# One level of Strassen's method for half of the up products of a spectral MLP kernel

## The chip, the cores and the metric

The kernel runs on one core of one Trainium2 chip. TensorE (PE; its weight loads are listed as PEld) multiplies matrices into PSUM, VectorE (DVE), ScalarE (ACT) and GpSimd (POOL) work on tiles in SBUF, and SyncE (SP) issues nearly all DMAs. The metric is the time of one execution in microseconds on the device. Before the change the median of three runs is 363.61 us (363.41 to 364.26).

## What is computed

The input x has 2048 rows of 512 numbers. Each row is normalized, and the result is the sum of x, a filter in the frequency domain and a two-layer network:

```
xn  = (x - mean) / sqrt(var + 1e-5)
A   = irfft2(rfft2(xn) * (w_r + 1j * w_i))          # over rows and columns
h   = xn @ w1 + b1                                  # w1: 512 x 1792
act = h * tanh(softplus(h))                         # Mish
out = x + A + act @ w2                              # w2: 1792 x 512
```

Inputs and outputs are float32. Every product of matrices is done with float16 pairs: a number is split in a high and a low half, and three matmuls (high x high, high x low, low x high) are added up in PSUM.

## The kernel before

The 2048 rows are four groups g of 512. F = 1792 is 14 blocks f of 128 (NFC). For each pair (g, f), numbered n = 14 g + f, there are four steps. up(n) (line 711) forms 128 x 512 values of h, transposed, in one PSUM bank: four blocks of the inner dimension times three passes, twelve matmuls of 512 columns (L727), with w1t as weights and the transposed rows xnT[g] as moving operand. mish(n) takes the bank on ScalarE (L738) into a tile hb, a_hi(n) writes the high half of the activation on ScalarE (L747), a_lo(n) the low half on VectorE (L750). down(n) (line 754) adds twelve matmuls of 512 columns to the four banks of group g. When a group is done, mlp_end(g) adds its four banks to the output rows (L792). The up products have two PSUM banks (pool ps_h), the down sums four (ps_a), the filter two (ps_f).

The filter is stream A: a first transform of the rows (s1, before), then for c = 0 to 3 the units p2_unit (psP), spectrum (products dre, dim, then some twenty operations on VectorE and GpSimd per half, ending in u, L424 and L425), dp_unit (psA) and ip_pair (psT), whose results go through memory (d_t) to the inverse s1_inverse and s1_inverse_pair (psY), near the end.

The program has two parts. In opening() and middle() the order of the instructions on every engine is the order in which they are written (tc.manual_schedule()). middle() interleaves down(0) to down(19) and up(14) to up(24) with the rows of groups 1, 2 and 3: row_in (normalized rows, high half on ScalarE, low half on GpSimd, L249), r.turn (a transposing DMA into xnT, L253), r.fold (sums and differences of row pairs for the transform, L230 to L235) and row_pair (the transform). The largest filter weight is looked for by max_wm (L443). After that a planner orders the work from priorities and its own costs. Two generators run against each other: mlp_rest (line 796) gives up or down steps, and stream_a gives steps of the filter; the list HALVES says how many up or down steps follow each step of the filter. mlp_rest keeps five activations between up and down. Some first matmuls of the filter are kept in program order.

DMAs wait in one queue on SP, in order. Tiles of one tag share a ring of buffers.

Of the kernel before, what the change touches and what calls it, by code (L numbers as in the profile page):

```python
# [41 lines left out]
def spectral_mlp_kernel(ctx, tc, x, wt, w0, w1, b1, w2, cT, cIT, cM, out):  # L42
# [21 lines left out]
    d_t = dp.tile([2, 64, 2, 32, 256], F16, tag="d_t", name="d_t")  # L64

# [46 lines left out]
    def turned(t, a):  # L112
        v = t.rearrange("p (b a e) -> p a b e", b=2, a=2)[:, a]
        return v[:, :, ::-1] if a else v

    def s1_mm_pair(k, eo, ps):
        psr = [t.rearrange("p (b a e) -> p a b e", b=2, a=2) for t in ps]
        for a in range(2):
# [3 lines left out]
                lambda r, c, h: turned(eo[c][:, h, :], a),  # L122
# [20 lines left out]

    class Rows:

        def __init__(self, g, x4):
# [5 lines left out]
            self.xT = xnT[g] = cp.tile([P, 2, 4, 512], F16, tag=f"xnT{g}", name=f"xnT_{g}")  # L152
            self.xh, self.xs, self.eo = {}, {}, {}
# [73 lines left out]
        def fold(self, j, engines):  # L227
# [4 lines left out]
            eo = self.eo[j] = [qp.tile([P, 2, D], F16, tag="q1", name=f"eo{q}_{self.g}_{j}") for q in range(2)]  # L232
            for q, v in ((0, t), (1, b)):
                nc.scalar.copy(eo[q][:, 0, :], v)
                engines[2 + q].tensor_sub(eo[q][:, 1, :], v, eo[q][:, 0, :])  # L235

        def full(self, s):
# [8 lines left out]
            )  # L246

# [16 lines left out]

    def pow2_of(name, am, n=1, out_tag=None):

        cl = sp.tile([P, n], F32, tag=f"cl{n}", name=f"cl_{name}", bufs=2)
        nc.vector.tensor_scalar(cl, am, 2.0**-60, None, op0=ALU.max)
        p2 = cp.tile([P, n], F32, tag=f"p2_{name}", name=f"p2_{name}")
        nc.vector.tensor_single_scalar(p2.bitcast(I32), cl.bitcast(I32), 0x7F800000, op=ALU.bitwise_and)  # L270
        return p2

    def scalars(name, src, factor, recip=False):
        o = cp.tile([P, 1], F32, tag=f"sc_{name}", name=f"sc_{name}")
        if recip:
            nc.vector.reciprocal(o, src)
            src = o
        nc.vector.tensor_scalar(o, src, factor, None, op0=ALU.mult)
        return o
# [67 lines left out]
    def w1_hi(k, a=0, b=2):  # L347
# [3 lines left out]
        )  # L351

# [81 lines left out]
    def load_w0():  # L434
        wmt[8] = sp.tile([P, 4, 2, 64], F32, tag="w0t", name="w0t")
# [4 lines left out]
    def max_wm(c):  # L440
        if c == 0:
            sc["mxw"] = sp.tile([P, 9], F32, tag="mxw", name="mxw")
        nc.vector.tensor_reduce(  # L443
            sc["mxw"][:, c : c + 1],
            wmt[c] if c == 8 else wmt.pop(c),
            axis=AX.XYZ if c == 8 else AX.X,
            op=ALU.max,
            apply_absolute_value=True,
        )
# [1083 lines left out]
```

## Time and profile before

| | |
|---|---|
| median of the runs | 363.61 us |
| span of the profiled execution, first to last instruction | 361.6 us |
| PE busy | 353.9 us (98%) |
| DVE busy | 278.5 us (77%) |
| ACT busy | 187.7 us (52%) |
| POOL busy | 47.8 us (13%) |
| bytes moved by DMA | 54.98 MB |

The page of the profile gives the profiled execution's time as its span; the runs are timed around the whole execution, so what lies before the first and after the last instruction is in them and not in the span. A row of a group reads: line, engine, operation, tiles written <- read, shapes, how often; then busy time and the mean of one in ns; then the engine's idle time ahead of these and what ended it. Rows by time give the start, the duration and the instruction. Rows by stretch give, for each engine, the busy time and the number of instructions in that stretch, then the granted clock, the DMA share and GB/s. A matmul's duration includes its way through the array; matmuls in a row start closer together than they last.

### The profile page before, as it was taken

To read this page: it belongs to the slowest core of one execution; us is meant where nothing else is said; L and a number is where in the kernel's file an instruction comes from. 1 tells how busy PE (TensorE), PEld (TensorE's weight loads), DVE (VectorE), ACT (ScalarE), POOL (GpSimd) and SP (SyncE) were. 2 spreads that over 40 slices of the span, in tenths; PEclk is the share of its full clock that TensorE was granted. 3 is DMA by queue.
4 is the path that set the end of the run, shared out by engine and by line. 5 is a ranking of instruction groups with operands and counts; after the bars stand their busy time and mean duration, and the time that the engine had idled before them with its cause. 6 is when DMAs were issued, how large, how long until landed. Compare 5 with 4: busy or idle time off the path is not lost.

```text
span 361.6 us, 6167 instructions
## 1 busy us (share of the span) xinstructions
PE 353.9 (98%) x2283; PEld 174.0 (48%) x2283; DVE 278.5 (77%) x543; ACT 187.7 (52%) x288; POOL 47.8 (13%) x49
## 2 busy tenths in 40 slices
PE   7999999999999999999999999999999999999994
PEld 2544444444444444545554445544554445444453
DVE  4898998886598776399998955996498933349995
ACT  5989974564654751525454365355443554445511
POOL 0020002303304500033030301130032000000000
PEclk9999999999999999999999999999999999999999
DMA  8945753699796657443611327218831524686566
GB/s 269 319 145 181 190 126 89 125 220 255 119 309 127 143 169 178 172 111 88 227 31 51 97 57 233 61 52 215 228 96 41 130 58 111 124 248 219 118 153 197
DMA packets 60702, 54.98 MB, mean 152 GB/s; under 512 B 16720, under 2 KB 49776, under 8 KB 60544
## 3 DMA queue, kind: packets, MB, share of 16 engines
q1 hardware_dynamic: 60192, 54.06, 56.6%
q10 hardware_dynamic: 480, 0.52, 0.5%
q8 instruction: 18, 0.29, 0.3%
q14 instruction: 12, 0.10, 0.1%
HBM read 34.61 MB, written 12.58 MB: 131 GB/s over the span
## 4 chain that ended last, share of the span: by engine, by line
PE 90%; DVE 6%; ACT 1%; DMA 1%; issue 0%; DVEq 0%
PE ph L727 39%; PE pa L68 13%; PE pa L71 12%; PE pa L72 12%; PE psT L672 2%; PE psS L108 1%; PE psY L108 1%; DMA x<-in_x_dram 1%; PE psA L68 1%; PE psA L71 1%; PE psA L72 1%; PE psP L516 1%; PE psP L526 1%; DVE u L425 1%; PE psP L519 1%; DVE xh L188 1%
## 5 line engine op out<-in xcount | busy, mean ns | idle before, releaser
L727 PE MATMUL ph<-xnT,w1t 128*128 128x512 f16 x672 | 153.4, 379 | 0.0
L727 PEld LDWEIGHTS <-w1t 128*128 128x128 f16 x672 | 64.6, 98 | 77.7 <-issue 2.7
L738 ACT ACTIVATE hb<-ph,b1t,fp_exp 128x512 f32<-128x512 f32 x56 | 43.2, 771 | 58.3 <-PE ph L727 58.2
L68 PE MATMUL pa<-w2t,a 128*128 128x512 f16 x181 | 68.7, 380 | 0.0
L71 PE MATMUL pa<-w2t,a 128*128 128x512 f16 x181 | 68.6, 379 | 0.0
L72 PE MATMUL pa<-w2t,a 128*128 128x512 f16 x181 | 68.6, 379 | 0.0
L750 DVE SCALAR_TENSOR_TENSOR a<-hb,ip_a,a 128x512 f16<-128x512 f32 x46 | 34.4, 749 | 34.4 <-ACT a L747 34.2
L747 ACT ACTIVATE a<-hb,ip_a 128x512 f16<-128x512 f32 x46 | 33.1, 720 | 2.3 <-DVE ip_a L288 1.2
L72 PEld LDWEIGHTS <-a 128*128 128x128 f16 x190 | 18.6, 98 | 21.0
L68 PEld LDWEIGHTS <-a 128*128 128x128 f16 x190 | 18.6, 98 | 20.8 <-issue 2.0
L71 PEld LDWEIGHTS <-a 128*128 128x128 f16 x190 | 18.6, 98 | 18.6
L249 POOL TENSOR_TENSOR xh<-xs,xh 128x512 f16<-128x512 f32 x12 | 15.4, 1292 | 56.7 <-ACT xh L223 23.4
L424 ACT ACTIVATE u<-w,sc_u 128x512 f16<-128x512 f32 x16 | 10.8, 713 | 22.1 <-DVE w L625 10.2
L531 DVE SCALAR_TENSOR_TENSOR z<-psP,z 128x512 f16<-128x512 f32 x16 | 10.8, 688 | 9.6 <-ACT z L530 9.6
L223 ACT ACTIVATE xh<-x,nb,rs 128x512 f16<-128x512 f32 x12 | 9.6, 806 | 13.1 <-DVE nb L217 11.7
L695 DVE SCALAR_TENSOR_TENSOR tt<-psT,tt 128x512 f16<-128x512 f32 x16 | 10.4, 683 | 7.3 <-ACT tt L694 7.3
L600 POOL TENSOR_TENSOR w<-X,wE 128x512 f32<-128x512 f32 x4 | 5.1, 1274 | 69.6 <-DVE X L593 69.6
L694 ACT ACTIVATE tt<-psT 128x512 f16<-128x512 f32 x16 | 8.8, 589 | 10.7 <-PE psT L672 8.8
L649 ACT ACTIVATE at<-psA 128x512 f16<-128x512 f32 x16 | 9.2, 589 | 9.4 <-PE psA L72 7.0
L156 DVE BATCH_NORM_STATS2 st<-x 128x6 f32<-128x512 f32 x16 | 10.3, 679 | 4.4 <-DMA x<-in_x_dram 4.4
L425 DVE SCALAR_TENSOR_TENSOR u<-w,sc_u,u 128x512 f16<-128x512 f32 x16 | 11.4, 747 | 2.4 <-ACT u L424 2.2
L530 ACT ACTIVATE z<-psP 128x512 f16<-128x512 f32 x16 | 9.4, 590 | 5.3 <-PE psP L526 5.2
(220 smaller groups left out, 576.7 us busy)
## 6 DMA issues: line engine op xcount, KB each, us to landing
d_y<-y SPq DMA_DIRECT2D x16, 256.0 KB, 4.2
wm<-in_wt_dram SPq DMA_DIRECT2D x8, 512.0 KB, 5.2
ai<-at SPq DMA_DIRECT2D x64, 64.0 KB, 2.2
d_t<-tt SPq DMA_DIRECT2D x32, 128.0 KB, 2.5
w1s<-in_w_dram SPq DMA_DIRECT2D x7, 512.0 KB, 9.0
w2s<-in_w_dram SPq DMA_DIRECT2D x7, 512.0 KB, 3.4
x<-in_x_dram SPq DMA_DIRECT2D x12, 256.0 KB, 7.4
yt<-d_y SPq DMA_DIRECT2D x6, 512.0 KB, 4.1
```

The lines of the kernel that those rows point to most:

```text
L68: first = nc.tensor.matmul(ps, stat(0), mov(0), start=start, stop=False)
L71: nc.tensor.matmul(ps, stat(0), mov(1), start=False, stop=False)
L72: nc.tensor.matmul(ps, stat(1), mov(0), start=False, stop=stop)
L249: engine.tensor_sub(self.xh[s][:, 1, :], self.xs[s], self.xh[s][:, 0, :])
L424: nc.scalar.activation(dst_h, src, AF.Copy, scale=scale)
L425: nc.vector.scalar_tensor_tensor(dst_l, src, scale, dst_h, op0=ALU.mult, op1=ALU.subtract)
L531: nc.vector.scalar_tensor_tensor(zl, psv, 2.0**-14, zh, op0=ALU.mult, op1=ALU.subtract)
L695: nc.vector.scalar_tensor_tensor(tt[:, :, 1, :], ps[r], 2.0**-12, tt[:, :, 0, :], op0=ALU.mult, op1=ALU.subtract)
L727: nc.tensor.matmul(ph[n + k], w1t[:, hw, dc, f * P : (f + 1) * P], xnT[g][:, hx, dc, :], start=(hw, hx, dc) == (0, 0, 0), stop=(hw, hx, dc ...
L738: nc.scalar.activation(hbt[n], ph.pop(n), AF.Mish, bias=b1t[:, f : f + 1], scale=s_exp[part_of(f)])
L747: nc.scalar.activation(act[n][:, 0, :], hbt[n], AF.Copy, scale=sc["a"])
L750: nc.vector.scalar_tensor_tensor(act[n][:, 1, :], hbt.pop(n), sc["a"], act[n][:, 0, :], op0=ALU.mult, op1=ALU.subtract)
```

## The change

The up products of groups 0 and 1 stay. For groups 2 and 3 (n from 28 on), one level of Strassen's method, in Winograd's form, is used: the 512 rows of a group are two halves of 256 (each half is one row of every pair), the 512 inner numbers are two halves, and the two blocks f = 2k and 2k + 1 of w1 are the other factor. Instead of eight products of 256 columns there are seven (six matmuls each: three passes times two inner blocks), on sums of row quarters (S1 to S4) and of weight quarters (T1 to T4).

unit(g, ks) does two such k at once, or one for the last, in four phases on two banks a and b. After each phase comes a down step. Banks are emptied and added on the way by ScalarE copies and VectorE sums:

```diff
+        with tc.manual_schedule(engines={PE}):
+            a, b = (ps_h.tile([P, n, 256], F32, tag="h", name=f"ph{c}_{g}_{ks[0]}") for c in "ab")
+            products(a, g, ks, "B11", "A11", True)
+            products(b, g, ks, "B21", "A12", True, True)
+        h1, h2 = (
+            mp.tile([P, n, 2, 256], F32, tag="hb", name=f"h{c}_{g}_{ks[0]}", bufs=2) for c in "12"
+        )
+        with tc.high_priority():
+            nc.scalar.copy(h1[:, :, 0, :], a)
+            nc.vector.tensor_add(h1[:, :, 0, :], h1[:, :, 0, :], b)
+        yield
+        with tc.manual_schedule(engines={PE}):
+            products(a, g, ks, "T2", "S2", False)
+            products(b, g, ks, "T1", "S1", True)
+        with tc.high_priority():
+            nc.scalar.copy(h2[:, :, 0, :], a)
+        yield
+        with tc.manual_schedule(engines={PE}):
+            products(a, g, ks, "T3", "S3", False)
+        with tc.high_priority():
+            nc.scalar.copy(h2[:, :, 1, :], a)
+            nc.vector.tensor_add(h2[:, :, 1, :], h2[:, :, 1, :], b)
+        yield
+        with tc.manual_schedule(engines={PE}):
+            products(a, g, ks, "T4", "A22", False, True)
+            products(b, g, ks, "B22", "S4", False, True)
...
+        for j in range(n):
+            mish_of(h1[:, j, 0, :], h1[:, j, 0, :], j, 0)
+        with tc.high_priority():
+            for j in range(n):
+                mish_of(h1[:, j, 1, :], a[:, j, :], j, 0)
+            nc.vector.tensor_add(h2[:, :, 0, :], h2[:, :, 0, :], b)
...
```

After the fourth phase come the Mish, a_hi and a_lo of all four blocks. mlp_rest runs the units:

```diff
+        for g in (2, 3):
+            for ks in ((0, 1), (2, 3), (4, 5), (6,)):
+                for k in ks:
+                    load_w1t(g, k)
+                last = g == 2 and ks[-1] == 6
+                for i, _ in enumerate(unit(g, ks)):
+                    if last:
+                        for name in ("A", "S", "O", "DT")[i]:
+                            load_ops(name)
+                    if len(ks) > 1:
+                        yield 1
+                        down_next()
+                    else:
+                        down_next((0, 1) if i % 2 == 0 else (2, 3))
+                    yield 1
```

The sums of the weights are made once from a second load of w1, on GpSimd, split in halves on ScalarE and VectorE, and stored in memory (d_w); each unit loads them again through a ring of three buffers:

```diff
+    def sums_w1(k, engine):
+
+        q = w1qs[k]
+        b11, b12, b21, b22 = q[:, 0:2, :P], q[:, 0:2, P:], q[:, 2:4, :P], q[:, 2:4, P:]
+        engine.tensor_sub(b11, b12, b11)
+        engine.tensor_sub(b12, b22, b12)
+        engine.tensor_sub(b22, b22, b11)
+        engine.tensor_sub(b21, b21, b22)
+
+    def store_w1t(k):
+        q = w1qs.pop(k)
+        th = cp.tile([P, 2, 4, 2 * P], F16, tag="T", name=f"wh_{k}", bufs=3)
+        split(th[:, 0], th[:, 1], q, sc["w1", w1_part(k)])
+        nc.sync.dma_start(d_w[k], th.rearrange("p h c f -> p (h c f)"))
+
+    def load_w1t(g, k):
+        wring[g, k] = cp.tile([P, 2, 4, 2 * P], F16, tag="T", name=f"wt_{g}_{k}", bufs=3)
+        nc.sync.dma_start(wring[g, k].rearrange("p h c f -> p (h c f)"), d_w[k])
```

Blocks 0 to 4 are done between the steps of middle(), 5 and 6 in stream A's first p2 units. The rows of groups 2 and 3 get their sums in middle() too, and go transposed into operands A, D, S, T, O; those of group 3 wait in memory (d_r) and are loaded, transposing, during group 2's last unit:

```diff
+        def sums(self, j):
+
+            a, b, sf = self.xs[2 * j], self.xs[2 * j + 1], self.sf
+            nc.vector.tensor_add(sf[:, 0, :], b[:, :256], b[:, 256:])
+            nc.vector.tensor_sub(sf[:, 1, :], sf[:, 0, :], a[:, :256])
+            nc.vector.tensor_sub(sf[:, 2, :], a[:, 256:], sf[:, 1, :])
+            nc.scalar.copy(self.sp[:, :, 0, :], sf)
+            nc.gpsimd.tensor_sub(self.sp[:, :, 1, :], sf, self.sp[:, :, 0, :])
```

Four of the eight maxima of the filter weights become sums of squares on ScalarE, and all are compared as squares:

```diff
-        nc.vector.tensor_reduce(
-            sc["mxw"][:, c : c + 1],
-            wmt[c] if c == 8 else wmt.pop(c),
-            axis=AX.XYZ if c == 8 else AX.X,
-            op=ALU.max,
-            apply_absolute_value=True,
-        )
+        t, m = wmt[c] if c == 8 else wmt.pop(c), sc["mxw"][:, c : c + 1]
+        if c != 8 and c % 2 == 0:
+            nc.scalar.activation(t, t, AF.Square, accum_out=m)
+            return
+        nc.vector.tensor_reduce(m, t, axis=AX.XYZ if c == 8 else AX.X, op=ALU.max, apply_absolute_value=True)
+        nc.vector.tensor_mul(m, m, m)
```

The residual rows of group 2 go to the ring "big" and are loaded when down(38) is done, the inverse's last four inputs are loaded later, and the tiles hb are two of double size instead of four. HALVES is unchanged.

More of the change, by code (lines that the diff above doesn't have):

```diff
@@ L794, in mlp_end @@
                 store_out(g, s, r)
[L796 to L810 removed]
+    STRASSEN = 2 * NFC
@@ L811, in mlp_rest, with down_next @@
+    def mlp_rest(n_up, n_down, lag):
+        def down_next(part=range(4)):
+            nonlocal n_down
+            down(n_down, part)
+            if 3 in part:
                 if n_down % NFC == NFC - 1:
@@ L1230, in row_in @@
     def row_in(r, s):
+        if r.g > 1 and s % 2:
+            r.hi_second(s)
+            r.full(s)
+            r.lo_second(s, POOL)
+            r.sums(s // 2)
+            return
         r.hi(s)
@@ L1325, in middle @@
             q.stats(s)
+        sums_w1(1, POOL)
         act_of(18)
```

296 lines of the change are left out of this document (226 added, 70 removed).

## The prediction

> **What bounds the kernel now.** I read the page's first part and its chain of waits, then the costliest groups, then the tensor engine's rows in order of time, then busy times stretch by stretch.
>
> ```profile
> span 361.6 us, 6167 instructions
> PE 353.9 (98%) x2283; PEld 174.0 (48%) x2283; DVE 278.5 (77%) x543; ACT 187.7 (52%) x288; POOL 47.8 (13%) x49
> PE 90%; DVE 6%; ACT 1%; DMA 1%; issue 0%; DVEq 0%
> ```
>
> TensorE is busy for 98% of the span and holds 90% of the chain, so a matmul that is left out is worth its place in the queue, if nothing else becomes late. The 77% of VectorE is a mean over very unequal stretches. In the next rows the columns are the stretch, its length, then PE, PEld, DVE, ACT and POOL busy.
>
> ```profile
> 82.00:140.00 58.00, 58.00 (x350) 26.69 (x349) 44.92 (x88) 29.26 (x44) 14.00 (x16) 1.00 0.77 181
> 153.70:182.40 28.70, 28.36 (x169) 14.09 (x167) 27.59 (x59) 11.36 (x20) 5.89 (x4) 1.00 0.44 134
> 182.40:211.90 29.50, 29.50 (x198) 15.26 (x195) 25.85 (x45) 14.58 (x24) 5.90 (x4) 1.00 0.28 73
> 211.90:223.30 11.40, 11.40 (x93) 6.06 (x92) 4.04 (x7) 5.24 (x10) 0.00 (x0) 1.00 0.51 134
> 223.30:251.10 27.80, 27.80 (x181) 14.14 (x179) 25.79 (x45) 13.99 (x23) 5.89 (x4) 1.00 0.38 109
> 251.10:261.60 10.50, 10.50 (x90) 5.61 (x88) 3.94 (x6) 5.07 (x9) 0.00 (x0) 1.00 0.92 239
> 261.60:288.60 27.00, 27.00 (x168) 13.22 (x166) 25.48 (x47) 12.29 (x20) 5.44 (x4) 1.00 0.38 91
> 288.60:320.30 31.70, 31.70 (x211) 15.03 (x209) 10.21 (x16) 12.85 (x20) 0.00 (x0) 1.00 0.46 107
> 323.10:357.90 34.80, 33.72 (x286) 17.78 (x284) 34.12 (x70) 13.24 (x20) 0.00 (x0) 1.00 0.66 186
> ```
>
> The first row is the hand-ordered middle. The four spectrum stages (153.7, 182.4, 223.3 and 261.6 on) leave VectorE 1.1, 3.6, 2.0 and 1.5 us idle; between them lie lighter stretches. In the last row, the inverse transforms and the ends of the sums, VectorE is free for 0.7 us in 34.8. So there are two engines near their limit, and the change relieves one and loads the other.
>
> **The TensorE saving.** The mean of 379 ns of a 512-column matmul includes its drain; what counts is the distance of starts.
>
> ```profile
> 346.01 0.38 PE L72 MATMUL pa<-w2t,a 128*128 128x512 f16 x1
> 346.23 0.27 PE L68 MATMUL psY<-yi_w,cITt 128*128 128x256 f16 x1
> ...
> 346.77 0.27 PE L72 MATMUL psY<-yi_w,cITt 128*128 128x256 f16 x1
> 346.88 0.38 PE L68 MATMUL pa<-w2t,a 128*128 128x512 f16 x1
> ```
>
> ```profile
> 159.59 2.60 PE ph L727 x12
> 175.25 1.42 DVE u L425 x2
> 176.66 0.61 DVE z L531
> ```
>
> Six 256-column matmuls take 346.88 - 346.23 = 0.65 us, 0.109 each; twelve of 512 take 2.60, 0.216 each. Half the columns cost half the time. Groups 2 and 3 have 28 blocks, 28 x 12 = 336 matmuls of 512, 336 x 0.216 = 72.6 us. They become 2 groups x 7 column pairs x 7 products x 6 = 588 matmuls of 256, 588 x 0.109 = 64.1. The saving is 8.5; with unrounded starts (0.2157 and 0.1092) 8.3, which I use. It comes at 1.18 per unit of two column pairs, nearly all of it in the third phase, which has only one product, and 0.59 in a unit of one.
>
> The other cost on this engine is 588 - 336 = 252 more weight loads.
>
> ```profile
> L727 PEld LDWEIGHTS <-w1t 128*128 128x128 f16 x672 | 64.6, 98 | 77.7 <-issue 2.7 <-ACT w1t L349 0.3
> ```
>
> ```profile
> 288.98 0.22 PE L68 MATMUL psA<-cMt,u 128*128 128x128 f16 x1
> ...
> 289.37 0.22 PE L71 MATMUL psA<-cMt,u 128*128 128x128 f16 x1
> ```
>
> psA has a fresh weight load for every 128-column matmul, and eight of them lie 289.37 - 288.98 = 0.39 us apart from first to last, 0.056 each. Loads of 98 ns are hidden even there, so I cost them at nothing under 0.109. If that cover is gone, each shows at most its 98 ns, 24.7 us in all. The Trainium skill (TensorE: Matmul & The Clock Gate, Part 3) says that a weight load overlaps running matmuls only when the row groups differ, which full-array products never do; by that rule the 24.7 us would be due. The 0.056 us spacing disagrees with it here.
>
> **What is added.** Durations come from these rows.
>
> ```profile
> L249 POOL TENSOR_TENSOR xh<-xs,xh 128x512 f16<-128x512 f32 x12 | 15.4, 1292 | 56.7 <-ACT xh L223 23.4 <-DVE xs L239 18.8 <-DMA cTt<-in_cT_dram 14.1
> L750 DVE SCALAR_TENSOR_TENSOR a<-hb,ip_a,a 128x512 f16<-128x512 f32 x46 | 34.4, 749 | 34.4 <-ACT a L747 34.2
> L888 DVE TENSOR_TENSOR m<-m,ys 128x512 f32<-128x512 f32 x12 | 7.9, 684 | 0.3 <-ACT ys L878 0.3
> L592 DVE TENSOR_TENSOR X<-dre,es 128x256 f32<-128x256 f32 x8 | 3.4, 422 | 6.7 <-ACT er L560 5.8 <-ACT es L553 0.9
> L355 DVE SCALAR_TENSOR_TENSOR w1t<-w1s,ip_w,w1t 128x1024 f16<-128x1024 f32 x7 | 9.0, 1283 | 1.0 <-ACT w1t L349 1.0
> L443 DVE TENSOR_REDUCE mxw<-wm 128x1 f32<-128x1024 f32 x8 | 9.5, 1210 | 0.0
> L601 DVE TENSOR_TENSOR w<-X,wO 128x512 f32<-128x512 f32 x4 | 5.9, 1486 | 0.0
> L603 DVE TENSOR_TENSOR w<-w,w 128x512 f32<-128x512 f32 x8 | 5.5, 684 | 0.1
> L694 ACT ACTIVATE tt<-psT 128x512 f16<-128x512 f32 x16 | 8.8, 589 | 10.7 <-PE psT L672 8.8 <-DMA ai<-at 1.9
> ```
>
> *Middle.* VectorE gets 12 row sums (0.42, 5.0), five low halves of the weight sums (1.28, 6.4), and loses four maxima to ScalarE (1.21, 4.8): +6.6 on 44.9, where 13.1 are free. GpSimd gets five blocks of four 256-wide subtractions (half of 1.29 each, 12.9) and the wide low halves of the row sums, less four shorter ones: some +18 on 14.0. L601, which runs beside a GpSimd product, takes 1.49 for work that L603 does in 0.68, so GpSimd company can double a VectorE operation with two inputs. Such operations fill about half of the 58 us (four folds of four operations at L603's 0.68, 11; the sums, 5.0; the weights' low halves, 6.4; nine a_lo, 6.7): half of the added 18 is up to 9 more. With 6.6 + 9 = 15.6 against 13.1 the middle could be 2.5 late. I take 0, since five activations lie ahead of the down products, each worth 2.60 us of TensorE's work, and keep 0 to +3. The Trainium skill (SBUF — State Buffer, Who interferes with whom) states it as a lock: a two-input VectorE instruction and a GpSimd instruction that reads block each other fully. L601 against L603 agrees; if all 18 us were met by it, an estimate, the middle would be late by 11.
>
> *Spectrum stages.* Each full unit adds three sums of 128x512 from a bank (0.68 by L888; L592 shows that reading a bank is no dearer) and three ScalarE copies (0.59, ScalarE is half idle). Its four low halves a_lo (0.75) come together after the fourth phase instead of one by one. By the places of the ups in the plan of before: stage one +2 sums, +1.28 for the low half of weight block 6, -3 a_lo = +0.4; stage two +4 sums, +2.6; stage three +2 sums, three half ones, one a_lo more, +3.3; stage four +3 sums, +2.0. TensorE's share shrinks by 1.2, 1.2, 1.8 and 1.2. VectorE then needs 28.0, 28.4, 29.1, 27.5 us where TensorE needs 27.5, 28.3, 26.0, 25.8: short by 0.5, 0.1, 3.1 and 1.7, 5.4 together. Work that isn't urgent can slip into the light stretches (7.4, 6.6 and 21.5 us idle), but the sums and the bank evictions can't. I take a third, 1.8; bounds 0 and 5.4.
>
> *Between the streams.*
>
> ```profile
> 307.82 6.85 SPq L700 DMA_DIRECT2D d_t<-tt  x8
> 316.61 1.92 SPq L857 DMA_DIRECT2D yi_z<-d_t  x4
> ```
>
> The last store of d_t is issued at 314.7 and the first reload at 316.6; the inverse begins at 320.3, right behind it. Up products lie over this transfer; the short third phase falls there, so TensorE arrives 1.2 early. I take half, 0.6; bounds 0 and 1.2.
>
> *Tail.* After 323 VectorE gets one full sum (0.68), three half ones (1.27) and, because the last full unit's four a_lo now come after its fourth phase, three more of them (2.25, at 0.67 by their spacing 2.0): 3.7 in all, with 0.7 free. What TensorE saves there (0.6) is worth nothing then. +3.0; bounds 0 and 3.7.
>
> *Transfers.*
>
> ```profile
> wE<-in_wt_dram SPq DMA_DIRECT2D x4, 512.0 KB, 5.7
> ```
>
> Fourteen 512 KB reloads of weight sums are new, some behind a ring slot that frees only after the fourth phase before; the second phase needs them 2.6 + 2.6 + 2.6 = 7.8 us later. At 5.7 they are hidden by 2.1. Each reload waits on SP's queue, with the spectrum's transfers behind it. I cost it at 0; if the cover is gone, up to 2 per unit.
>
> **Sum.** 361.6 - 7.7 (the saving ahead of the tail) + 1.8 + 0.6 + 3.0 = 359.3 us of span. The runs' median is 363.61, 2.0 above this execution's span; I leave that as it is: 361.3.
>
> **The rivals.**
>
> *All of it arrives (0.13).* The planner slips VectorE's work into its idle time in the tail too: 363.6 - 8.3 = 355.3, or 358.3 with the tail's 3.0 paid. For it: 98% PE. Against: the tail's 0.7 us.
>
> *VectorE becomes the bound (0.28).* Place: the spectrum stages and the tail; price: 5.4 + 1.2 + 3.7 and up to 3 in the middle, 10.3 to 13.3 against 7.7: 366.2 to 369. It decides slower once the waits ahead of the tail exceed 4.7. For it: the chain already runs through VectorE before 177 (the rows at 175.25 and 176.66 above). Against: the seven rows from 153.7 to 320.3 hold 43.6 us of idle VectorE against 8.3 us added.
>
> *Banks and buffers are held too long (0.13).* A unit keeps two banks and both h buffers for four phases; between third and fourth lie only a down product's 2.6 us for a 0.59 copy.
>
> ```profile
> ACT u L424 <- DVE w L625: 10.2, 2, 5.2
> ```
>
> ScalarE can stand 5.2 us behind a VectorE wait, and the copy behind it then stops TensorE for 5.2 + 0.6 - 2.6 = 3.2. Once in most stages costs about 3 us over the sum: 363.5 to 365, no change or a little slower.
>
> *The short matmuls cost more than half (0.02)*, by visible weight loads: 363.6 - 8.3 + 24.7 = 380.
>
> **How the numbers follow.** The forecast has the remaining 0.44, with 359.5 to 363 as its own range. What a measurement of this kernel tells from no change is 0.2%, 0.7 us. Faster: 0.13 and 0.41 of the forecast's, 0.02 of the banks', 0.56; same: 0.03, 0.06 of the banks', 0.04 of VectorE's, 0.13; slower: 0.24 + 0.05 + 0.02 = 0.31. The range 357.0 to 367.5 reaches to both sides.
>
> **What would show it.** Right: matmuls of 128x256 on w1 spaced 0.109 us, PE gaps gathered in the spectrum stages, DVE over 34 in the last 35 us, that stretch longer by 3. Wrong: no PE gaps at all (355), gaps right before the phases' first matmuls with ScalarE as releaser (banks), gaps before 140 (GpSimd), gaps released by weight reloads (the ring).

## The result and the profile after

The changed kernel takes 420.05 us (418.8 to 420.58) where the kernel before, beside it, takes 363.62: a ratio of 1.154, with an interval of 1.152 to 1.157. I had predicted 361.3, with a range up to 367.5. The forecast was wrong in sign, and the upper end of the range was missed by 52.6 us.

From the page of the changed kernel: the span, busy times, the slices of PE and of the granted clock (40 slices of 10.4 us, in tenths), and the chain of work that ended last.

```profile
span 417.0 us, 6930 instructions
PE 363.9 (87%) x2535; PEld 203.6 (49%) x2535; DVE 311.3 (75%) x585; ACT 216.4 (52%) x345; POOL 75.8 (18%) x81
PE   8999999999399879866699899989958989979794
PEclk9999999999979989989989999999997999999999
DVE 32%; PE 21%; DMA 14%; ACT 13%; issue 7%; POOL 7%; SPq 5%; DVEq 0%; ACTq 0%; POOLq 0%
```

TensorE, 98% busy and 90% of the chain before, is 87% busy and 21% of the chain. VectorE's share of its span even fell (77% to 75%). So no engine took TensorE's place as the bound. The chain now hops between six engines and queues. Its members wait for one another, and the holes in the PE line begin in the eleventh slice, at 104 us, inside the hand-ordered middle.

Two rows of the tensor engine in order of time, the first forward product psP and the first inverse product psY, show how late each is. Of the kernel before:

```profile
143.76 0.22 PE L68 MATMUL psP<-cMt,yt 128*128 128x128 f16 x1
...
320.29 0.85 PE L108 MATMUL psY<-yi_z,cITt 64*64 64x256 f16 x24
```

Of the changed kernel:

```profile
163.45 0.23 PE L70 MATMUL psP<-cMt,yt 128*128 128x128 f16 x1 [0.47 <-DMA yt<-d_y]
...
373.61 0.30 PE L110 MATMUL psY<-yi_z,cITt 64*64 64x256 f16 x2 [2.25 <-DMA yi_z<-d_t]
```

The middle is 19.7 us late. Between it and the inverse another 33.6 are lost: psP of the second column block begins 29.6 us late, that of the third 38.3, that of the fourth 40.3, psY 53.3. The last matmul starts at 411.55 against 356.61, 54.9 late. The largest losses thus lie in the middle, in the first two spectrum stages and just before the inverse.

The waits of the changed kernel between 95 and 165 us (waiter, what it waits for; us in total, times, longest):

```profile
POOL w1q L419 <- DMA w1q<-in_w_dram: 21.0, 4, 9.8
ACT wh L505 <- POOL w1q L422: 14.2, 4, 4.9
DVE wh L506 <- ACT wh L505: 10.4, 4, 5.8
...
PE psS L110 <- ACT eo L263: 4.6, 4, 1.8
...
PE pa L70 <- DVE m L888: 3.4, 1, 3.4
```

In the kernel before, the same view of TensorE is empty from 95 to 150 us. The first three lines are one chain: GpSimd waits for a load, ScalarE for GpSimd, VectorE for ScalarE. TensorE's 4.6 us for eo stand behind it, as the next rows show. The 3.4 us in the last line needn't come from that load: without any weight sums the same wait is 2.8 us in e1 and 3.0 in e5 below, and 0.5 in e11, which has no row sums either. The order of time of the changed kernel shows one pass of the chain (start, length, engine; in brackets the idle time before and what ended it):

```profile
94.00 1.26 SPq L157 DMA_TRANSPOSE xT<-zr  x1
...
95.31 0.58 SPq L413 DMA_DIRECT2D w1q<-in_w_dram  x1
...
99.85 0.72 POOL L419 TENSOR_TENSOR w1q<-w1q 128x256 f32<-128x256 f32 x1 [3.43 <-DMA w1q<-in_w_dram]
...
102.95 0.67 POOL L292 TENSOR_TENSOR zr<-xs,zr 128x256 f16<-128x256 f32 x1
103.02 1.15 ACT L505 ACTIVATE wh<-w1q,ip_w 128x1024 f16<-128x1024 f32 x1 [3.71 <-POOL w1q L422]
103.57 1.64 POOL L301 TENSOR_TENSOR zr<-zr 128x768 f16<-128x768 f32 x1
...
104.08 0.76 ACT L822 ACTIVATE hb<-ph,b1t,fp_exp 128x512 f32<-128x512 f32 x1
104.20 2.09 DVE L506 SCALAR_TENSOR_TENSOR wh<-w1q,ip_w,wh 128x1024 f16<-128x1024 f32 x1 [5.76 <-ACT wh L505]
...
104.89 2.75 PE L809 MATMUL ph<-xnT,w1t 128*128 128x512 f16 x12 [1.57 <-ACT hb L822]
...
108.78 0.62 ACT L263 CAST eo<-xe 128x512 f16<-128x512 f32 x1 [2.22 <-DVE xe L251]
...
109.45 0.27 PE L110 MATMUL psS<-eo,cTt 64*64 64x256 f16 x1 [1.81 <-ACT eo L263]
```

The first weight block is issued on SP only at 95.31, behind transposing loads. GpSimd stands 3.43 us for it, and the rows' low halves (L292, L301) stand behind its four subtractions. ScalarE has stood 3.71 us for GpSimd, VectorE 5.76 for ScalarE, with everything that the hand order places behind them. Behind ScalarE's wh stands the Mish at 104.08, and TensorE's up product waits 1.57 us for it; behind VectorE's wh stands xe, and TensorE's transform waits 1.81 us for eo.

### The profile page after: what moved, and what is told of

The parts are those of the page before. It is cut to its first block, busy times and chain, and to the rows that moved or that the text cites. A ratio compares the mean times of both kernels' runs of the same rounds, so it can differ in the third digit from the quotient of the medians.

```text
span 417.0 us, 6930 instructions
## 1 busy us (share of the span) xinstructions
PE 363.9 (87%) x2535; PEld 203.6 (49%) x2535; DVE 311.3 (75%) x585; ACT 216.4 (52%) x345; POOL 75.8 (18%) x81
## 4 chain that ended last, share of the span: by engine, by line
DVE 32%; PE 21%; DMA 14%; ACT 13%; issue 7%; POOL 7%; SPq 5%; DVEq 0%; ACTq 0%; POOLq 0%
DMA wt<-d_w 4%; PE pha L898 4%; PE phb L898 3%; PE pa L70 3%; PE pa L73 3%; PE pa L74 3%; DMA yi_z<-d_t 2%; ACT a L831 2%; DMA w1q<-in_w_dram 2%; DVE a L834 2%; DVE st L177 2%; DVE y L135 2%; DVE w2t L500 1%; ACT wh L505 1%; DVE wh L506 1%
## 5 line engine op out<-in xcount | busy, mean ns | idle before, releaser
L809 PE MATMUL ph<-xnT,w1t 128*128 128x512 f16 x336 | 75.7, 379 | 3.7 <-ACT hb L822 3.6
L898 PEld LDWEIGHTS <-wt 128*128 128x128 f16 x336 | 32.7, 100 | 15.3 <-DMA wt<-d_w 4.4
L961 ACT ACTIVATE h<-h,b1t,fp_exp 128x256 f32<-128x256 f32 (+1 forms) x28 | 18.7, 702 | 15.3 <-DVE h L941 11.7
L834 DVE SCALAR_TENSOR_TENSOR a<-h,ip_a,a 128x512 f16<-128x512 f32 x28 | 20.8, 767 | 7.4 <-ACT a L831 7.1
L822 ACT ACTIVATE hb<-ph,b1t,fp_exp 128x512 f32<-128x512 f32 x28 | 21.4, 765 | 4.7 <-PE ph L809 3.9
L834 DVE SCALAR_TENSOR_TENSOR a<-hb,ip_a,a 128x512 f16<-128x512 f32 x18 | 14.5, 809 | 9.3 <-ACT a L831 8.9
L505 ACT ACTIVATE u<-w,ip_u 128x512 f16<-128x512 f32 x16 | 10.7, 714 | 20.5 <-DVE w L707 9.4
L506 DVE SCALAR_TENSOR_TENSOR wh<-w1q,ip_w,wh 128x1024 f16<-128x1024 f32 x7 | 9.8, 1399 | 15.2 <-ACT wh L505 15.2
L831 ACT ACTIVATE a<-h,ip_a 128x512 f16<-128x512 f32 x28 | 19.4, 717 | 0.3
L70 PE MATMUL psA<-cMt,u 128*128 128x128 f16 x64 | 11.8, 224 | 8.5 <-DVE at L732 8.5
```

The costliest lines, as they stand in the source:

```text
L70: first = nc.tensor.matmul(ps, stat(0), mov(0), start=start, stop=False)
L505: nc.scalar.activation(dst_h, src, AF.Copy, scale=scale)
L506: nc.vector.scalar_tensor_tensor(dst_l, src, scale, dst_h, op0=ALU.mult, op1=ALU.subtract)
L809: nc.tensor.matmul(ph[n + k], w1t[:, hw, dc, f * P : (f + 1) * P], xnT[g][:, hx, dc, :], start=(hw, hx, dc) == (0, 0, 0), stop=(hw, hx, dc ...
L822: nc.scalar.activation(hbt[n], ph.pop(n), AF.Mish, bias=b1t[:, f : f + 1], scale=s_exp[part_of(f)])
L831: nc.scalar.activation(act[n][:, 0, :], hbt[n], AF.Copy, scale=sc["a"])
```

## What the idle gaps cost beside their length

The tensor engine's rows after one such gap, changed kernel:

```profile
115.08 0.59 PE L70 MATMUL pa<-w2t,a 128*128 128x512 f16 x1 [3.37 <-DVE m L888]
115.46 0.63 PE L73 MATMUL pa<-w2t,a 128*128 128x512 f16 x1
...
119.70 0.38 PE L74 MATMUL pa<-w2t,a 128*128 128x512 f16 x1
119.92 0.38 PE L809 MATMUL ph<-xnT,w1t 128*128 128x512 f16 x1
```

And the busy times around it (stretch, length, PE, PEld, DVE, ACT, POOL, then the granted clock, the DMA share and GB/s), changed kernel:

```profile
109.40:112.80 3.40, 1.31 (x24) 0.78 (x24) 3.32 (x7) 3.15 (x6) 0.00 (x0) 1.00 0.95 277
112.80:119.70 6.90, 4.62 (x12) 1.62 (x11) 6.80 (x17) 2.37 (x4) 3.23 (x4) 0.51 1.02 314
```

After 3.37 us without a matmul the starts lie 0.43 us apart instead of 0.216, until 119.70, where the 0.22 returns. The granted clock is 0.51 from 112.8 to 119.7. The Trainium skill (TensorE: Matmul & The Clock Gate, Part 1: The HAM clock gate) says that the array drops to half its clock after about one idle window of 3.4 us and needs a busy window of the same length to come back. The half clock agrees with these rows, the idle window doesn't: the clock fell at 112.8, 1.1 us into the pause, after 3.4 us in which TensorE had still been busy for 1.31. In e5, below, it fell with no long pause at all, after three holes of 0.59 to 0.75 us:

```profile
124.60:128.00 3.40, 1.45 (x12) 0.60 (x14) 3.15 (x5) 2.42 (x4) 3.40 (x5) 1.00 0.37 134
128.00:131.40 3.40, 3.40 (x25) 1.57 (x25) 3.01 (x5) 1.42 (x3) 2.17 (x6) 0.50 0.01 2
```

So short holes close together are enough. I counted every matmul of 256 or 512 columns after the start-up that is followed without a pause at 1.85 to 2.1 times the usual distance: 47 in the changed kernel and none in the kernel before. Their excess is 7.1 us. At most an eighth of the loss is thus idle time's aftermath; how much of it reaches the span isn't measured.

## The experiments

Theory Q: the loss comes from the preparation, through engines and a DMA queue that work in order. Theory V: VectorE has become the bound. Theory B, later H: TensorE waits for the up banks. Theory R: the row sums' own arithmetic is late in the middle. The expectations name the others. Most of these kernels leave a part of the computation out or put other data in its place, as the text on each says, so their times measure parts and aren't versions. Each was timed beside the kernel before (363.5 to 363.7 us in the four groups of runs). Behind the middle the planner orders each of these kernels anew, so a difference there holds its new order too.

**e1, no weight sums.** Loading, summing, splitting, storing and reloading of the weight sums are left out; the products that need them take plain blocks of w1.

```diff
 def load_w1q(k):
+    return
 def sums_w1(k, engine):
+    return
 def store_w1t(k):
+    return
...
-                w = lambda h, dc: t[:, h, c0 + dc, o : o + P]
+                w = lambda h, dc: w1t[:, h, c0 + dc, 2 * k * P + o : 2 * k * P + o + P]
```

> Leaves out the weight sums altogether: no second load of w1, no subtractions on GpSimd, no split and store, no reloads; the units read plain blocks of w1t in their place, so the result is not the reference's. TensorE's work, the row sums, the bank copies and VectorE sums of the units stay. Theory Q (queues: the middle and the first spectrum stage wait in order behind load, GpSimd, ScalarE, VectorE, store and reload of the weight sums): nearly all of the 56 us goes, 362 to 375. Theory V (VectorE is overloaded by the units' sums): only the seven low halves of 1.28 leave VectorE, 405 to 412. Theory B (banks and h buffers held by a unit): the units are the same, 410 or more outside the middle, so 395 to 405.

Measured 388.62 us, ratio 1.069 (1.066 to 1.072): 31.4 back, more than V and B allowed and 13.6 short of Q's range. The weight sums are the larger part of the loss and not nearly all of it.

**e2, sums stored but not reloaded.** Only the fourteen reloads go, and the products that need them take plain blocks of w1 as in e1:

```diff
-                for k in ks:
-                    load_w1t(g, k)
```

> Weight sums are made and stored as in the changed kernel, but never loaded again: the units read plain blocks of w1t, so the result is not the reference's. Theory Q: the preparation costs some 20 us in the middle and up to 20 in the first spectrum stage, the reloads the rest; so 395 to 408. If the reloads were the cause instead of the preparation: 370 or less. Theories V and B: 412 to 420, as before.

Measured 413.1 us, 1.136 (1.133 to 1.140). The reloads cost 420.05 - 413.1 = 7.0 us, and making and storing the sums 413.1 - 388.6 = 24.5. The time lies in the range that V and B gave, above Q's: Q had put more on the reloads. Where the 24.5 arise, psP's first rows tell: in e1 it begins at 152.37, in e2 at 163.66, so 11.3 us are lost in the middle. At the second column block it is 175.87 against 196.80, another 9.6 by the end of the first spectrum stage, in which weight blocks 5 and 6 are made.

**e3, e1 without the staging of group 3's operands**, which reads group 2's instead:

```diff
 def operand(g, name):
+    g = 2
...
-            else:
-                o, w = OPERANDS[name]
-                nc.sync.dma_start(d_r[j, :, o : o + w], src)
...
-                        for name in ("A", "S", "O", "DT")[i]:
-                            load_ops(name)
```

> As the kernel without weight sums, and besides nothing of group 3's row operands goes through memory: no stores of them in the middle, no transposing loads in group 2's last unit; group 3's units read group 2's operands, so the result is not the reference's. If the ten transposing loads of 1.2 us each on SP's queue delay the filter's weights (the GpSimd product waited 28 us for one), this is 6 to 13 us faster than without the weight sums alone; if not, within 2 us of it.

Measured 383.33 us, 1.054 (1.051 to 1.058): the staging costs 5.3, a little under the 6 that I had set as the sign of it. What it does to the queue shows in the changed kernel's DMA issues on SP:

```profile
283.13 3.74 SPq L157 DMA_TRANSPOSE xA<-d_r  x2
...
295.99 2.52 SPq L157 DMA_TRANSPOSE xD<-d_r  x2
298.61 2.52 SPq L157 DMA_TRANSPOSE xT<-d_r  x2
301.18 0.58 SPq L432 DMA_DIRECT2D wt<-d_w  x1
301.86 2.60 SPq L782 DMA_DIRECT2D d_t<-tt  x4
304.50 0.61 SPq L582 DMA_DIRECT2D wE<-in_wt_dram  x1
```

A transposing load, of 256 or 128 KB here, holds SP for 1.26 us against 0.58 for a plain load of 512 KB. Ten of them, the spectrum's stores between and one reload stand ahead of the last stage's filter weights wE. GpSimd stands 28.0 us for wE, but in the kernel before, too, it stood up to 20.9 us at a time, without delaying TensorE. What reaches TensorE goes through VectorE, which waits for wE and then for g, a load further back in SP's queue; the psA products wait for at, which stands behind both on VectorE:

```profile
309.80 0.69 DVE L681 TENSOR_TENSOR w<-X,wE 128x512 f32<-128x512 f32 x1 [5.80 <-DMA wE<-in_wt_dram]
312.35 0.76 DVE L654 TENSOR_TENSOR r<-g,c0t 4x256 f32<-4x256 f32 x1 [1.86 <-DMA g<-es]
...
314.83 0.27 PE L70 MATMUL psA<-cMt,u 128*128 128x128 f16 x1 [7.16 <-DVE at L732]
```

This is TensorE's longest pause in the changed kernel. In e1 the same place has 5.48 us; in e3 no pause behind the middle is longer than 1.7.

**e4, all preparation, plain up products.** Row sums, weight sums, stores and group 3's staging stay; the up products of groups 2 and 3 are the twelve matmuls of 512 columns of before, and units, copies, VectorE's bank sums and reloads are gone.

```diff
-        while n_up < STRASSEN:
+        while n_down < len(UP) - LAST:
...
+        return operand(g, "AS"[hx]).rearrange("p n e -> p (n e)")[:, 512 * dc : 512 * dc + 512]
```

> All preparation of the changed kernel (row sums, weight sums, stores, group 3's transposing loads) stays, but groups 2 and 3 run the old up products of twelve 512-column matmuls on whatever lies in the row operands, with no units, no bank copies, no VectorE sums and no reloads; the result is not the reference's. Theory Q: the preparation alone makes this slower than the kernel before, 395 to 410. Theories V and B: without units it comes back to 365 to 372.

Measured 398.92 us, 1.097 (1.094 to 1.101). Preparation without any unit costs 35.4 us: theory Q carries most of the loss. e2, which has the same preparation with the units, takes 14.2 more, though its TensorE work is 8.3 less.

**e5, row sums only, plain up products.** e4 without weight sums and staging, or e3 without units. Against e4:

```diff
 def load_w1q(k):
+    return
 def sums_w1(k, engine):
+    return
 def store_w1t(k):
+    return
 def operand(g, name):
+    g = 2
...
-            else:
-                o, w = OPERANDS[name]
-                nc.sync.dma_start(d_r[j, :, o : o + w], src)
...
-                if n_up == 3 * NFC:
-                    for name in "ASODT":
-                        load_ops(name)
```

> As the kernel before in its products (groups 2 and 3 form their up products by twelve matmuls of 512 columns, no weight sums, no units, no copies or sums of banks), but with the row sums and differences of groups 2 and 3 kept and their transposes made; group 3 reads group 2's operands, nothing is staged. It is e3 with plain up products in place of the seven. Theory U (the row sums cost what the middle shows, 151.9 - 143.8 = 8.1 us, and nothing behind it; the rest of e3 is lost inside the units): 363.5 + 8.1 = 371.6, from 370 to 373. Theory M (the row sums leave a backlog on VectorE and GpSimd that also delays the stages behind the middle): 377 to 383.

Measured 371.81 us, 1.023 (1.020 to 1.026): theory U's number. Row sums, with all that is left of the change beside them, cost 8.3 us, and what e3 has above that, 11.5, is lost in the units.

**e6, units without copies and bank sums.**

```diff
-        with tc.high_priority():
-            nc.scalar.copy(h1[:, :, 0, :], a)
-            nc.vector.tensor_add(h1[:, :, 0, :], h1[:, :, 0, :], b)
...
-            mish_of(h1[:, j, 0, :], h1[:, j, 0, :], j, 0)
+            mish_of(h1[:, j, 0, :], a[:, j, :], j, 0)
...
-            mish_of(hbt[m], hbt[m], j, 1)
+            mish_of(h2[:, j, 0, :], b[:, j, :], j, 1)
+            mish_of(h2[:, j, 1, :], b[:, j, :], j, 1)
```

> e3 without the copies of bank a and without the three VectorE additions of each unit: Mish reads the two banks directly when all seven products are done, so what is computed in the units is not the product; the matmuls are all there. Takes 24 additions (14.6 us of VectorE) and 24 copies (12.6 us of ScalarE) away and with them every wait of TensorE inside a unit. From the first forward product to the last matmul e3 takes 224.2 us, the kernel before 212.8, and 8.3 fewer are due: 19.7 us are lost there. Theory V (VectorE is what is short) and theory B (TensorE waits for banks to be copied and for the h tiles) both expect most of the 19.7 back: 364 to 370. If it stays above 377, the loss in the units is not theirs but the matmuls' own (short products, their operands) or ScalarE's.

Measured 379.67 us, 1.044 (1.041 to 1.047): only 3.7 back, where V and B had expected most of 19.7.

**e7, copies kept, bank sums left out.** Against e3:

```diff
-            nc.vector.tensor_add(h1[:, :, 0, :], h1[:, :, 0, :], b)
-            nc.vector.tensor_add(h2[:, :, 1, :], h2[:, :, 1, :], b)
-            nc.vector.tensor_add(h2[:, :, 0, :], h2[:, :, 0, :], b)
```

> e3 with the three VectorE additions of each unit left out and the copies of bank a kept (so the halves lack M2, M6, M7's share and the result is not the product). 14.6 us of VectorE go; TensorE still waits for every copy of bank a before it starts the next product in it. Theory V: about 14.6 / (14.6 + 7.5 of longer residual) of the loss, 10 to 14 us back: 369 to 373. Theory B: only the release of bank b gets faster, 1 to 5 us back: 378 to 382.

Measured 378.24 us, 1.040 (1.037 to 1.043): 5.1 back, at the upper edge of B and half of what V asked for. It is 1.4 faster than e6, which leaves out the copies as well, so these parts don't simply add up.

**e8, no low halves in groups 2 and 3.** The down products use the high half twice.

```diff
             a_hi(m)
-            a_lo(m)
+            hbt.pop(m)
```

> e3 without the low half of the activations of groups 2 and 3 (28 instructions, 21.0 us of VectorE); the down products of these groups use the high half twice, so TensorE does the same work on other data. The banks, copies and additions of the units stay. Theory V: VectorE's relief of 21.0 us is more than e7's 14.6, so it gains more: 364 to 371. Theory B: the units' banks are waited for as before, 0 to 5 us back: 378 to 383.

Measured 383.91 us, 1.056 (1.049 to 1.063): nothing, although VectorE has 28 instructions less. Busy times between 165 and 335 us (columns as above), of e3 and then of e8:

```profile
165.00:335.00 170.00, 160.10 (x1297) 104.48 (x1295) 131.39 (x236) 85.90 (x150) 20.47 (x15) 1.00 0.40 109
```

```profile
165.00:335.00 170.00, 159.74 (x1303) 104.70 (x1304) 116.65 (x214) 85.29 (x151) 20.58 (x15) 1.00 0.41 111
```

VectorE has 14.7 us less to do in these 170 and TensorE is no busier. Theory V falls: VectorE's load isn't what holds the units up, though its sums, as steps between two products in a bank, cost the 5.1 of e7. Who waits shows in TensorE's waits from 165 us on, of e3:

```profile
PE phb L898 <- DVE h L952: 3.6, 3, 1.4
PE psY L110 <- DMA yi_z<-d_t: 2.0, 2, 1.7
PE psT L754 <- DVE X L677: 1.9, 2, 1.1
PE pa L70 <- DVE m L888: 1.3, 2, 1.0
PE pha L898 <- ACT h L951: 1.0, 1, 1.0
...
```

The whole list adds up to 14.1 us, and the units' banks (phb, pha) are a third of it. The rest are waits of the spectrum's, the inverse's and the down products for other engines. In e5, with plain blocks in the same places, the same view has one line, 0.3 us for psP.

**e9 and e10, the saving without its structure.** To measure what 8.2 us less of TensorE work is worth, 38 of the 336 up matmuls of groups 2 and 3 are left out, one or two at the end of each block, in e5 (e9) and in the kernel before (e10).

```diff
+        if n >= 2 * NFC:
+            steps = steps[: -2 if n % NFC in (1, 4, 7, 10, 13) else -1]
```

> e5 (row sums kept, plain up products) with 38 of its 336 up matmuls in groups 2 and 3 left out, one or two at the end of each block: 38 x 0.216 = 8.2 us less TensorE work, as much as the seven products save, without their structure. Theory H (the saving can be had; what loses it in e3 is that a unit holds both banks of the up products from its first matmul to its last Mish): 371.8 - 8.2 = 363.6, from 362.5 to 366. Theory C (the stages are set by the other engines, and TensorE's work is only their cover): 368 to 372.

> The kernel before with the same 38 up matmuls of groups 2 and 3 left out and nothing else changed. It measures what 8.2 us less of TensorE work is worth where all stands as before. Theory H: 363.5 - 8.2 = 355.3, up to 357.5. Theory C: 359 to 363.5.

Measured 367.47 us for e9, 1.010 (1.007 to 1.013), 4.3 below e5; and 358.47 for e10, 0.986 (0.983 to 0.989), 5.2 below before. Both lie between the theories: 53 to 64% of the work taken away arrives as time. TensorE's waits from 150 us on, e10, show where the rest goes:

```profile
PE psP L516 <- DVE z L531: 1.2, 1, 1.2
PE dre L68 <- DVE at L650: 0.5, 1, 0.5
PE psY L108 <- DMA yi_z<-d_t: 0.4, 1, 0.4
PE psA L72 <- DVE u L425: 0.4, 1, 0.4
```

As soon as TensorE gets shorter it waits at four places, 2.5 us in sum, where it had waited at one, 0.3 us for psP.

**e11, e5 without the row sums' arithmetic.** Three VectorE additions, a copy and a GpSimd subtraction per pair of rows go; the transposes stay and carry the rows.

```diff
         def sums(self, j):
-            a, b, sf = self.xs[2 * j], self.xs[2 * j + 1], self.sf
...
+            return
```

> e5 without the arithmetic of the row sums: per pair of rows three additions on VectorE, a copy on ScalarE and a subtraction on GpSimd are left out; the transposes that carried the sums carry the rows instead, and the halves of the odd rows are still split as in e5. Theory R (VectorE's extra work in the middle, 6.6 us by the prediction's count, is what makes it 8.1 us late): most of the 8.1 comes back, 363.5 to 366.5. Theory Q (the order of the queues is, whatever VectorE does: transposing loads and GpSimd's low halves): 369 to 372.

Measured 365.4 us, 1.005 (1.003 to 1.007): 6.4 of the 8.3 back, in theory R's range. The middle's busy times, of e5 and then of e11:

```profile
82.00:148.00 66.00, 61.09 (x353) 27.93 (x352) 50.45 (x104) 35.28 (x56) 19.25 (x20) 0.97 0.66 152
```

```profile
82.00:148.00 66.00, 65.48 (x393) 30.39 (x392) 44.75 (x102) 34.33 (x55) 12.50 (x17) 1.00 0.78 182
```

In e5 TensorE stands still for 4.9 us of the 66, with VectorE busy for 50.5, free for 15.5. A free share didn't help. The added instructions stand between others in a written order, and what is behind them is late: TensorE waits 3.0 us for the group's end (pa for m) and 1.9 for eo in e5, and 0.5 in all in e11. The edit takes work from VectorE, ScalarE and GpSimd at once, so it doesn't tell whose instructions matter most.

**e12, one bank per unit.** e6 with units of one pair, all seven products in one bank, and two Mish of 512 columns from it.

```diff
-            a, b = (ps_h.tile([P, n, 256], F32, tag="h", name=f"ph{c}_{g}_{ks[0]}") for c in "ab")
+            t = ps_h.tile([P, 2, 256], F32, tag="h", name=f"ph{g}_{ks[0]}")
+            a, b = t[:, 0:1, :], t[:, 1:2, :]
...
-            for ks in ((0, 1), (2, 3), (4, 5), (6,)):
+            for ks in ((0,), (1,), (2,), (3,), (4,), (5,), (6,)):
```

> e6 (no copies, no additions of banks) with units of one pair of blocks instead of two, all seven products of a unit into one bank of 512 columns, and two Mish of 512 columns reading that bank: the same 588 matmuls of 256 columns, but the second up bank is free while a unit runs, as with plain blocks. What the banks hold isn't the product. Theory H: the loss in the units ends, 379.7 goes to 363 to 368. Theory C: nothing changes by the banks, 375 to 380.

Measured 371.12 us, 1.020 (1.017 to 1.024): 8.6 below e6, 3.6 above e9. Most of the structure's cost goes when the other bank is free; theory H's range is missed by 3. The edit has a second effect: it also takes 28 of e6's 56 Mish instructions away, so the 8.6 are not the banks' alone. In e6's trace only 1.4 of TensorE's waits behind 165 us are at a bank; how a held bank costs the rest, the waits don't show. The 8.6 aren't the short matmuls' either: e12 has all 588 of them.

**e13, e14 and e15, what in the weight sums costs 24.5.** All are e2 with a part left out: e13 the loads (the subtractions take halves of w1 that are in SBUF), e14 the arithmetic (the loaded weights are stored as they are), e15 GpSimd's subtractions only.

```diff
 e13, load_w1q
-        nc.sync.dma_start(w1qs[k], w1[:, 2 * k * P : (2 * k + 2) * P].rearrange("(c p) f -> p c f", p=P))
 e14, store_w1t
-        split(th[:, 0], th[:, 1], q, sc["w1", w1_part(k)])
-        nc.sync.dma_start(d_w[k], th.rearrange("p h c f -> p (h c f)"))
+        nc.sync.dma_start(d_w[k], q.rearrange("p c f -> p (c f)"))
 e14 and e15, sums_w1
+        return
```

> e2 (weight sums prepared and stored, never loaded again; 413.1) without the seven loads of raw weights: the four subtractions take the weights that are already in SBUF as halves, the split goes with a constant scale, and the stores stay, so the sums are not the right ones. Theory L (GpSimd waits for a load that SP issues late, and ScalarE, VectorE and TensorE wait behind it): most of the 24.5 us between e2 and e1 comes back, 389 to 397. Theory A (the arithmetic in the engines' queues costs it): 405 to 412.

> e2 with the loads of raw weights and the stores kept, and without the subtractions on GpSimd and the split on ScalarE and VectorE: the stores write the loaded weights. The same 512 KB move each way. Theory L2 (the loads and stores alone disturb SP's queue and the spectrum's transfers): 405 to 413. Theory L (a load is only harmful because GpSimd waits for it and the others wait behind GpSimd) and theory A: 389 to 395.

> e2 without GpSimd's 28 subtractions; loads, splits on ScalarE and VectorE and stores stay (the raw weights are split). ScalarE now waits for the load itself. Theory L: the wait for a late load moves from GpSimd to ScalarE, so little comes back: 403 to 413. If GpSimd's own queue is what matters (its low halves of the rows and the filter's products held behind the sums): 392 to 400.

Measured 403.38 us for e13 (1.110, 1.105 to 1.115), 393.36 for e14 (1.082, 1.079 to 1.085) and 401.41 for e15 (1.104, 1.101 to 1.108). e14 lies where L and A put it; e13 and e15 each fall between the two ranges. Loads and stores alone cost 393.4 - 388.6 = 4.7; arithmetic and stores without loads cost 14.8; together they cost 24.5, 5 more than the two apart. So theory L, my first reading of the waits, is too narrow. The late load makes it worse, but the arithmetic in the queues, with the stores, costs three times as much as the transfers, and GpSimd's 28 subtractions are 11.7 of it. Of the 24.5 up to 6.9 are the slow clock: by the same count as above the excess of slow matmuls is 10.9 us in e2 and 4.0 in e1.

**e16, real units of one pair.** Against e3:

```diff
-            for ks in ((0, 1), (2, 3), (4, 5), (6,)):
+            for ks in ((0,), (1,), (2,), (3,), (4,), (5,), (6,)):
```

> e3 with units of one pair of blocks instead of two: all products, copies and additions are there, but a unit holds its two up banks for about 4.6 us of TensorE instead of 9.2, with 14 units instead of 8 and so 42 instead of 24 copies and additions of half the width. Theory H (held banks cost 8.5 of e6's time): shorter holding helps, 375 to 381. If the number of hand-overs between TensorE and the copies is what costs: 386 to 392.

Measured 387.95 us, 1.067 (1.060 to 1.075): 4.6 slower than e3. This is in the range of the hand-overs. TensorE's waits from 165 us on, of e16:

```profile
PE phb L898 <- DVE h L952: 6.5, 4, 2.2
PE pha L898 <- ACT h L939: 4.2, 2, 2.1
PE pha L898 <- ACT h L951: 4.2, 3, 1.6
```

With two smaller lines the waits at the units' banks are 16.4 us, where e3 has 4.6: with the real copies and additions, more hand-overs cost more than shorter holding saves. Between two phases stands half a down product here where e3 has a whole one, so each hand-over also has less cover. H was too simple: the copies and sums between the products cost by their number. What e6 loses without them, these runs don't divide further.

**The path from before to after.** Each step is the difference of two kernels, with the planner's new order in it; the sum is closed by construction, and a step in another order could differ (without units, weight sums and staging together cost 398.9 - 371.8 = 27.1, with them 29.8).

| step | kernels | us |
|---|---|---|
| wider transposes, split odd rows, and the rest of the change (filter maxima, later loads) | before to e11 | +1.8 |
| arithmetic of the row sums | e11 to e5 | +6.4 |
| 8.2 us less TensorE work | e5 to e9 | -4.3 |
| the units' structure, no copies or sums | e9 to e6 | +12.2 |
| copies and VectorE sums of banks | e6 to e3 | +3.7 |
| staging of group 3's operands | e3 to e1 | +5.3 |
| making and storing the weight sums | e1 to e2 | +24.5 |
| reloading them | e2 to after | +7.0 |

None of these kernels with the row sums beats the kernel before: the most that 8.2 us less of TensorE work brought is e10's 5.2, and the row sums alone, placed as they are, cost 8.3. No run places them elsewhere in the middle or changes HALVES, so what another order would recover stays open.

## Why the prediction was wrong

*The TensorE saving* was right as work and wrong as time. The rows of the changed kernel have twelve 256-column products in 1.47 us, the last one's drain of 0.27 included, so 0.109 apart:

```profile
218.98 1.47 PE L898 MATMUL phb<-xA,w1t 128*128 128x256 f16 x12
```

In such rows the 252 more weight loads cost nothing, as forecast. But I took 7.7 of the 8.3 off the span and then added stalls by hand; e10 shows 5.2 for the same work in an otherwise unchanged kernel. The share lost there, 3 us, is more than my 1.8 + 0.6 for all stages, with nothing added to any engine.

*The middle* is the step that failed most: "I take 0, since five activations lie ahead of the down products". By psP's first row it measured +8.5 with the row sums alone (152.25 in e5) and +19.7 in all. I compared the engines' added work (6.6, 18) with their free time (13.1 on VectorE), as if work could move into free time. In a middle whose order is written by hand it can't: e5 lost time with 15.5 us of VectorE free. The five activations cover TensorE only as long as their own steps aren't behind the wait, and act_of's Mish and high half stand on ScalarE behind wh, which stands behind GpSimd (the rows at 103.02, 104.08 and 104.89). I also counted how long GpSimd works and not what it waits for: 21.0 us for w1q. The contention that I had weighed is there: the wh at 104.20 took 2.09 us beside GpSimd's L301, where the low half of a weight block took 1.28 before. The lock of the Trainium skill (SBUF — State Buffer, Who interferes with whom) agrees in kind with that row; the estimate of 11 from it was nearer to the middle's 19.7 than my 0, though it prices only the lock and not the queues.

*Transfers*: "I cost it at 0; if the cover is gone, up to 2 per unit". The reloads measured 7.0, within that bound over eight units, so the bound was right and the 0 wrong. Both halves of what I named show in the waits: TensorE waits 3.6 us for a reload, and SP itself stands for a ring slot, with whatever follows in its queue:

```profile
SPq L432 <- PE pha L898: 8.4, 2, 7.8
```

How the 7.0 divide between the two isn't measured. The raw weights' loads and the stores (4.7 alone) were not priced. Group 3's staging (5.3) I hadn't costed at all; its ten transposing loads are moved into the place where the last stage needs SP.

*The spectrum stages*, costed at 1.8 as a shortage of VectorE, were wrong in kind. For weight block 6 I had put 1.28 us of VectorE into the first stage; blocks 5 and 6 are both made there, and with the weight sums the stage is 9.6 longer. e8 relieved VectorE and gained nothing. The units cost 12.2 + 3.7 = 15.9 us against plain blocks with the same TensorE work. The rival of banks and buffers held too long named this, at "about 3 us over the sum"; e12 points to it with up to 8.6, and 3.6 of the 12.2 stay unexplained.

*Between the streams*, 0.6: e3, without the preparation, waits 2.0 us for yi_z. *The tail*, +3.0: from the first inverse product to the last matmul it takes 411.55 - 373.61 = 37.9 us after and 356.61 - 320.29 = 36.3 before, +1.6, and +4.0 in e3. Both were of the right kind; the first was above its bound of 1.2. The tail's own addition was wrong as well: 0.68 + 1.27 + 2.0 is 3.95, not 3.7.

Of the rivals, VectorE's (366.2 to 369) and the weight loads' (380) had the sign, by the wrong mechanism, and none came near 420. Two of the signs that I listed as showing me wrong came true: gaps before 140 us, and gaps behind weight reloads (the page has PEld waiting 4.4 us for wt<-d_w). What failed in the method was to price each addition by its length against an engine's mean idle time, and to price nothing for its place in a queue.

## What to carry to other kernels

In a kernel like this one, whose bound engine is 98% busy and whose other engines' work is placed in its shadow, a saving on that engine can be worth less than its length (here 53 to 64%), and added work costs by where it stands in each in-order queue, not by the free share of its engine. Follow each new instruction through the queues: what it waits for, what stands behind it, and who waits for that. Before a transform like Strassen's is built, drop as many matmuls from the existing kernel as it would save: that one run tells what the saving brings in the order as it stands, and here it was less than the row sums alone cost.

## What the runs showed of the hardware

A pause of 3.37 us on TensorE was followed by 4.6 us of matmuls at 0.43 us instead of 0.216, at a granted clock of 0.51 over the stretch; in e5 three holes of 0.59 to 0.75 us within 3.4 us were followed by 3.4 us at 0.50. The kernel before has no such stretch, the changed one loses 7.1 us in them, e2 10.9. Stalls, and short ones close together too, can therefore cost more than they measure, which no term of my sum had. An issue of a transposing load occupies SP's queue for 1.26 us where a plain load of 512 KB takes 0.58, so ten of them, of 256 or 128 KB each, hold up whatever follows by more than their bytes suggest.
